# The start of a fused attention and feed-forward kernel rebuilt: two queues for q, column maxima of k by elementwise steps, exchanges on TensorE

## The chip, the cores and the metric

The kernel runs on one core of a Trainium2 chip. The metric is the device time of one execution in microseconds (us); three executions of the kernel before took 808.61, 810.38 and 810.49 us, so the median is 810.38.

## The reference

q, k and v are 8 batches x 8 heads x 576 rows x 64 columns. q goes through a softmax along its 64 columns, k through one along its 576 rows; for each batch and head the output is softmax(q) (softmax(k)ᵀ v). The heads are laid side by side, which gives x with 4608 rows of 512. Then out = softplus(x w_in) w_out with 2048 inner columns.

```python
q_s = softmax(q, axis=-1); k_s = softmax(k, axis=2)      # in fp32, with 1e-9 in the sums
kv  = einsum('bhsd,bhse->bhde', k_s, v)
x   = einsum('bhsd,bhde->bhse', q_s, kv)  ->  (4608, 512)
out = softplus(x @ w_in) @ w_out                          # (4608, 512)
```

## The kernel before

The 4608 rows are 9 tiles of 512. Tiles 0 to 2 go alone ("solo"): for each of 16 chunks j of the inner columns, U (line 720, `up`) makes a 512-wide product in PSUM with 12 matmuls, A (softplus, ScalarE) takes it out, G or H splits it into a high and a low part, and O (line 747, `down`) adds its product with w_out in 12 more matmuls. Every product is three matmuls, high x high, low x high, high x low. Chunks 0 and 1 of tile 0 are not split and go in plain fp32 (`up_whole`, line 707: tokens B and U1). Tiles 3 to 8 go as three pairs, by a scheme with 7 products for 8 (tokens C for the first matrix, e, t and d for the second). Weights come as 64-bit numbers and are decoded for each chunk: T and M (ScalarE), S, J and Q (mostly VectorE), P (ScalarE). Work on tile 0 can begin when q's softmax for it, and k's and v's part for batch 0, are done: that is the head, the part that the change rebuilds.

The order of everything is written out by hand: `ORDER` is a string of tokens, and `do` (line 1090) issues the instructions of each token as it comes. Each engine executes its own instructions in that order, and waits in place for what it needs. DMAs go mainly from SyncE's queue (SP), which is one line as well: a DMA that waits for a buffer holds up those behind it.

In the head before, SP loads q of tile 0 in four pieces of 64 partitions x 4 KB (`q_fetch`, line 555; z is the half of the partitions, g the pair of heads) and then the four k and v tiles of batch 0; their last 64 rows come from ScalarE's queue (`kv_load`, line 443). q (`q_unit`, line 570) takes a maximum over 32 columns, swaps the halves of each 64 over by four copies on ScalarE, and joins them for both pairs of heads at once; then it shifts, takes the exponential, sums, exchanges the sums by a matmul with the table `pair`, inverts and divides, half of each large step on VectorE and half on GpSimd. For k, `turn` (line 484) transposes the whole 128 x 10 x 64 tile on TensorE by ten matmuls into PSUM, and `across` takes the row maximum there with three VectorE steps. `spread` (line 506) sends the maximum back, `shift`, `power`, `product` and `scale` follow. The tokens w are matmuls on a table, with no use but to keep TensorE busy. Then q's transposes (`flip`, line 682), the product with kv (`x_product`, line 644), the copies to x0 (`take`, line 689), and U and O begin.

Of the kernel before, what the change touches and what calls it, by code (L numbers as in the profile page):

```python
# [7 lines left out]
F32 = mybir.dt.float32  # L8
# [11 lines left out]
P = 128  # L20
# [37 lines left out]
    k1.0.5 J4 U1 A0 k1.0.6 x0.2.3 k1.0.7 x0.2.4 O0 J3 P2 Q2 x0.0.3 x0.0.4 x0.1.3 T5 x0.3.3 x0.1.4 k1.1.1 x0.3.4 k1.1.2
    P3 Q3 A1 M5 k1.0.8 U2 T8 k1.1.3 k1.1.4 U3 P4 A2 q1.0 S5.1 T9 Q4 A3 G2 M6.1 O1 J5 G3 U4 k1.1.5 P5 O2 T6 M8.1 Q5.1
    k1.1.6 M7.1 T7 k1.2.0 k1.2.1 J6 J8 P6 k1.1.7 k1.2.2 q1.1 U5 A4 Q6 A5 J7 O3 U6 G4 G5 P7 M10 Q7 k1.1.8 O4 M9 q1.2  # L60
    T12 k1.3.0 U7 S9 q1.3 P8 A6 Q8 J9 T11 T10 A7 G6 q1.4 k1.3.1 O5 D4 P9 k1.2.3 G7 S10 M14.1 k1.2.4 q1.6 k1.3.2 O6
    M11.1 Q9 k1.2.5 U8 J11 A8 J10 P10 Q10 T14 U9 q1.8 A9 G8 M12.1 k1.2.6 k1.3.3 O7 P11 M13.1 Q11 J12 k1.3.4 G9 T13 P12
    q1.5 J13 q1.7 U10 Q12 J14 O8 U11 k1.3.5 A10 O9 k1.3.6 k1.2.7 U12 P13 A11 T15 Q13 q1.9 G10 q1.11 q1.10 P14 O10
    x1.0.0 A12 G11 U13 Q14 M15.1 k1.2.8 J15 x1.2.0 k1.3.7 P15 k1.3.8 Q15.1 U14 x1.1.0 A13 G12 D3 x1.1.3 O11 x1.3.0 U15
    G13 x1.0.4 x1.1.4 O12 x1.1.5 A14 x1.0.5 P0 Q0.1 k2.0.0 D6 G14 x1.3.3 D5 x1.2.4 k2.1.0 O13 x1.2.5 x1.3.4 P1 L2
    x1.3.5 D0 A15 Q1.1 G15 O14 k2.0.1 U16 k2.0.2 A16 D15 O15 U17 U18 A17 G16 k2.1.1 q2.1 Y0.1 k2.1.2 O16 G17 Y1.0 Y0.0
    q2.0 U19 k2.0.3 O17 A18 k2.1.3 k2.0.4 D1 G18 k2.1.4 Y0.2 D2 k2.0.5 q2.2 q2.3 Y1.2 D12 k2.1.5 Y2.1 A19 q2.5 O18
    Y1.1 D9 k2.1.6 k2.0.6 G19 D10 k2.0.7 q2.4.1 U20 Y2.0 Y2.2 n O19 U21 Y1.3 Y2.3 A20 Y0.3 D13 k2.0.8 Y2.4 Y2.5 G20
    Y1.4 O20 k2.2.0 U22 Y3.0 k2.1.7 A21 k2.2.1 D7 G21 k2.2.2 q2.6 q2.8 Y0.4 Y0.5 Y2.6 n D8 U23 q2.7 A22 k2.1.8 k2.2.3
    k2.3.0 Y3.2 O21 U24 G22 k2.3.1 k2.2.4 A23 q2.9 Y0.6 k2.3.2 A24 O22 q2.10 k2.3.3 k2.2.5 L3 Y1.5 H1.7.0 q2.11 x2.0.0  # L70
    D11 D14 k2.3.4 Y3.1 Y2.7 H1.7.1 U25 k2.2.6 k2.3.5 Y4.0 k2.2.7 Y2.8 k2.3.6 Y4.1 Y3.3 A25 Y1.6 O23 H1.8.0 U26 Y0.7
    k2.3.7 n A26 U27 Y3.4 x2.1.0 Y3.5 x2.2.0 H1.9.0 H1.8.1 O24 A27 Y3.6 H1.9.1 q3.0 O25 Y3.7 k2.3.8 k2.2.8 Y4.2
    H1.10.0 k3.0.0 n R0.0 Y3.8 H1.11.0 U28 k3.1.0 H1.10.1 x2.1.3 A28 q3.1 Y5.0 Y4.3 q3.12 x2.1.4 O26 Y0.8 Y4.4 k3.0.4
    H1.12.0 U29 q3.2 x2.1.5 U30 q3.3 k3.1.4 Y4.5 x2.0.4 H1.11.1 O27 x2.0.5 H1.12.1 A29 Y1.7 A30 U31 x2.3.0 H1.13.0
    x2.3.3 H1.13.1 k3.0.5 k3.1.5 q3.5 O28 q3.4 Y6.0 x2.3.4 Y7.1 R0.1 Y7.0 O29 x2.2.4 x2.2.5 R0.2 R0.3 q3.7 x2.3.5
    H1.14.0 Y6.1 L4 y0.1 H1.14.1 q3.6 A31 y0.0 R2.0 k3.1.6 Y7.2 k3.0.6 k3.0.7 Y1.8 Y6.2 Y4.6 q3.8 O30 H1.15.0 H1.15.1
    U32 n O31 n q3.13 y0.2 y1.0 A32 Y7.3 F1.0 Y4.7 U33 Y6.3 Y7.4 F1.2 Y6.4 q3.9 H2.0.0 k3.2.0 F1.3 y0.3 k3.3.0 R0.4
    y1.1 k3.2.4 A33 H2.1.0 U34 H2.0.1 F1.1 O32 k3.1.7 k3.2.5 k3.1.8 q4.0 q3.10 H2.1.1 y0.4 Y6.5 k3.0.8 y0.5 O33 k3.3.4
    A34 y1.2 k3.3.5 y2.0 k3.2.6 H2.2.0 Y4.8 q3.11 k3.3.6 H2.2.1 k3.2.7 U35 U36 R0.5 R0.6 y0.6 q4.1 Y7.5 A35 x3.1.0 n
# [131 lines left out]
def tile_attn_ffn(  # L211
# [249 lines left out]
    def kv_unit(b, h, bank):  # L461
# [10 lines left out]
        def top():  # L472
            if not b:
                return
# [95 lines left out]
    def q_unit(t):  # L570
# [48 lines left out]
        def invert():  # L619
            if t:  # L620
                if "s" not in state:
                    swap_all()
# [593 lines left out]
```

## Time and profile before

| | us |
|---|---|
| median of three executions | 810.38 |
| the profiled execution's own time | 809.8 |
| its span, first to last instruction | 808.0 |
| TensorE busy in the span | 795.7 (98%) |
| VectorE busy | 581.9 (72%) |
| ScalarE busy | 499.7 (62%) |
| GpSimd busy | 119.6 (15%) |

Names in the rows: PE is TensorE, DVE VectorE, ACT ScalarE, POOL GpSimd, SP SyncE; a q behind a name (SPq, ACTq) is its queue of DMAs. L with a number is the line of the kernel. `x` with a number is how many instructions a row merges. The duration of a row of several is from the first one's start to the last one's end. Instructions of one engine overlap at their ends, so the step from one start to the next is what an instruction costs in a row of them.

### The profile page before, as it was taken

How to read it: one execution, taken by the hardware profiler on the slowest of the kernel's cores; microseconds unless marked ns; L12 is line 12 of the kernel's file. 1: busy time of each engine (PE TensorE's matmuls, PEld its weight loads, DVE VectorE, ACT ScalarE, POOL GpSimd, SP SyncE). 2: the span in 40 equal slices, each digit the busy share in tenths (PEclk: the TensorE clock that was granted, in tenths of full speed). 3: DMA queues.
4: the chain of work that ended last, by engine and by line, in shares of the span. 5: the costliest groups of instructions: out<-in, count | busy, mean ns of one | idle time of the engine just before them, and what ended most of it. 6: DMA issues, size and time to landing. Idle time of an engine off the chain costs nothing.

```text
span 808.0 us, 12020 instructions
## 1 busy us (share of the span) xinstructions
PE 795.7 (98%) x4312; PEld 637.7 (79%) x4312; DVE 581.9 (72%) x934; ACT 499.7 (62%) x826; POOL 119.6 (15%) x211
## 2 busy tenths in 40 slices
PE   7999999999999999999999999999999999999997
PEld 6668877887787878878788778887777888888886
DVE  6979764877799878549689898477688943136884
ACT  2999964674577557557768574658466633336651
POOL 1320021101011210001010004240000220400026
PEclk9999999999999999999999999999999999999999
DMA  9996176869788898889789448994483865858655
GB/s 302 360 323 239 30 238 260 307 207 343 256 279 279 290 334 294 292 244 294 233 247 303 151 166 251 299 283 158 141 259 124 262 196 178 266 175 287 193 159 88
DMA packets 118235, 193.73 MB, mean 240 GB/s; under 512 B 8416, under 2 KB 90592, under 8 KB 108960
## 3 DMA queue, kind: packets, MB, share of 16 engines
q1 hardware_dynamic: 114912, 186.67, 70.0%
q0 software_dynamic: 2944, 6.04, 3.6%
q8 instruction: 34, 0.56, 0.3%
q10 hardware_dynamic: 320, 0.26, 0.1%
q14 instruction: 25, 0.20, 0.1%
HBM read 149.95 MB, written 42.99 MB: 239 GB/s over the span
## 4 chain that ended last, share of the span: by engine, by line
PE 94%; DMA 2%; ACT 1%; issue 1%; DVE 1%; POOL 0%; SPq 0%; DVEq 0%
PE po L965 7%; PE po L967 6%; PE po L966 6%; PE po L851 6%; PE po L853 6%; PE po L852 6%; PE po L766 5%; PE ph L724 5%; PE ph L725 5%; PE ph L726 5%; PE po L768 5%; PE po L767 5%; PE ph L851 3%; PE ph L853 3%; PE ph L852 3%; PE ph L965 3%
## 5 line engine op out<-in xcount | busy, mean ns | idle before, releaser
L1010 POOL DMA_DIRECT2D out<-w x92 | 59.4, 653 | 232.0 <-DVE w L1002 230.5
L766 PE MATMUL po<-w,g_hi 128*128 128x512 f32 x164 | 65.6, 400 | 0.0
L724 PE MATMUL ph<-x,w 128*128 128x512 f32 x164 | 65.3, 398 | 0.0
L945 ACT CAST g_hi<-w 128x512 fp32r<-128x512 f32 x74 | 45.8, 621 | 29.8 <-PE po L966 17.2
L768 PE MATMUL po<-w,g_lo 128*128 128x512 f32 x164 | 64.0, 390 | 0.0
L767 PE MATMUL po<-w,g_hi 128*128 128x512 f32 x164 | 64.0, 390 | 0.0
L726 PE MATMUL ph<-x,w 128*128 128x512 f32 x164 | 63.9, 390 | 0.0
L725 PE MATMUL ph<-x,w 128*128 128x512 f32 x164 | 63.9, 390 | 0.0
L948 DVE TENSOR_TENSOR g_lo<-w,g_hi 128x512 fp32r<-128x512 f32 x74 | 50.1, 684 | 11.4 <-ACT g_hi L945 11.1
L742 DVE TENSOR_TENSOR g_lo<-g,g_hi 128x512 fp32r<-128x512 f32 x46 | 32.7, 712 | 32.1 <-ACT g_hi L739 32.1
L733 ACT ACTIVATE g<-ph 128x512 f32<-128x512 f32 x48 | 28.6, 599 | 39.3 <-PE ph L726 39.1
L932 DVE TENSOR_TENSOR w<-w,w 128x512 f32<-128x512 f32 x72 | 47.5, 683 | 5.6 <-ACT w L885 5.6
L479 POOL PARTITION_ALL_REDUCE mx<-mx x20 | 23.0, 1150 | 189.6 <-DVE mx L476 186.4
L874 DVE TENSOR_TENSOR w<-po,w 128x512 f32<-128x512 f32 x24 | 16.3, 684 | 45.6 <-PE po L853 24.7
L945 ACT CAST w<-w 128x512 fp32r<-128x512 f32 x52 | 31.8, 619 | 22.5 <-PE po L966 14.8
L851 PE MATMUL po<-w,x 128*128 128x512 f32 x112 | 44.2, 394 | 0.3 <-DMA x<-sums 0.3
L852 PE MATMUL po<-w,x 128*128 128x512 f32 x112 | 43.6, 389 | 0.0
L853 PE MATMUL po<-w,x 128*128 128x512 f32 x112 | 43.6, 389 | 0.0
L948 DVE TENSOR_TENSOR w<-w,w 128x512 fp32r<-128x512 f32 x52 | 35.3, 684 | 10.9 <-ACT w L945 10.7
L739 ACT CAST g_hi<-g 128x512 fp32r<-128x512 f32 x46 | 28.3, 620 | 21.2 <-PE po L767 14.0
L476 DVE TENSOR_REDUCE mx<-kvt 128x128 f32<-128x640 f32 x28 | 36.7, 1312 | 5.6 <-DMA kvt<-in_kv_tail 4.4
L766 PEld LDWEIGHTS po<-w,g_hi 128*128 128x128 f32 x164 | 30.8, 188 | 10.2 <-issue 1.7
(380 smaller groups left out, 2253.2 us busy)
## 6 DMA issues: line engine op xcount, KB each, us to landing
x<-sums SPq DMA_DIRECT2D x24, 1024.0 KB, 5.6
kvt<-in_kv SPq DMA_DIRECT2D x30, 512.0 KB, 6.8
kept<-w SPq DMA_DIRECT2D x15, 1024.0 KB, 8.8
w<-kept SPq DMA_DIRECT2D x13, 1024.0 KB, 7.1
x<-sums_out SPq DMA_DIRECT2D x44, 256.0 KB, 4.3
w<-kept SPq DMA_DIRECT2D x36, 256.0 KB, 5.4
x<-kept SPq DMA_DIRECT2D x36, 256.0 KB, 4.8
w<-sums_out SPq DMA_DIRECT2D x36, 256.0 KB, 5.3
```

The lines of the kernel that those rows point to most:

```text
L724: nc.tensor.matmul(ph, lhsT=w_hi, rhs=x_hi, start=h == 0, stop=False)
L725: nc.tensor.matmul(ph, lhsT=w_lo, rhs=x_hi, start=False, stop=False)
L726: nc.tensor.matmul(ph, lhsT=w_hi, rhs=x_lo, start=False, stop=h == HP - 1)
L766: nc.tensor.matmul(po, lhsT=g_hi[:, ms], rhs=w_hi, start=j == 0, stop=False)
L767: nc.tensor.matmul(po, lhsT=g_hi[:, ms], rhs=w_lo, start=False, stop=False)
L768: nc.tensor.matmul(po, lhsT=g_lo[:, ms], rhs=w_hi, start=False, stop=j == NJ - 1)
L851: nc.tensor.matmul(ph, lhsT=w_hi, rhs=x_hi, start=c == 0 and i in (0, 4), stop=False, **more)
L852: nc.tensor.matmul(ph, lhsT=w_lo, rhs=x_hi, start=False, stop=False, **more)
L853: nc.tensor.matmul(ph, lhsT=w_hi, rhs=x_lo, start=False, stop=c == 1, **more)
L945: nc.scalar.copy(ring[p, i, s][0], right_of(p, i, s))
L948: engine.tensor_tensor(out=lo, in0=right_of(p, i, s), in1=hi.bitcast(F32), op=ALU.subtract)
L965: nc.tensor.matmul(bank, lhsT=w_hi, rhs=hi, start=begin, stop=False, **more)
```

## The change

- q of tile 0: the pieces of the upper 64 partitions (z = 1) go on ScalarE's queue, those of the lower on SP's.
- A new `q_first` for tile 0: each step by pairs of heads (g = 0, 1), with the halves of the maximum exchanged by a matmul with a new table `other_half` into PSUM, where four ScalarE copies did it.
- k's column maximum for batch 0: three elementwise maxima over the five chunks (two at a time, then the two results, then the last 64 rows), one 128 x 128 transpose on TensorE, and one row maximum. The ten matmuls of `turn` are gone.
- The inverses of k's sums are made for two heads at a time.
- The eight fills of batch 0's padding go from VectorE to GpSimd, ahead of GpSimd's first computing instruction, which has a token (g) of its own now.
- `ORDER` is written anew from the first token to the last. The token w stands for 25 table matmuls now (9, 5, 2, 5, 4) and 38 before (20, 5, 6, 7). The main products, their number and shapes, are the same.

```diff
-    w0.20 b0 b1 q0.0 n k0.0.1 n q0.1 n n q0.2 q0.3 q0.4.1 l0 q0.5 l1 k0.0.2 k0.1.1 l2 k0.1.2 k0.0.3 k0.2.1 k0.0.4
+    w0.9 b0 b1 n n n n g q0.0 q0.1 q0.2 q0.3 q0.4 w1.5 k0.0.0 q0.6 k0.0.1 q0.5 k0.1.0 l0 q0.7.1 k0.1.1 k0.0.2 k0.2.0
...
+    other_half = const.tile([P, P], F32, name="other_half")
...
+        nc.vector.tensor_tensor(out=other_half, in0=pair, in1=ident, op=ALU.subtract)
...
         def top():
+            mx = state["mx"] = sm.tile([P, 2, D], F32, name="mx", bufs=3)
             if not b:
+                two = sm.tile([P, 2, 2, D], F32, name="two")
+                for o, i0, i1 in (
+                    (two, kt[:, 0:2], kt[:, 2:4]), (mx, two[:, 0], two[:, 1]), (mx[0:TAIL], mx[0:TAIL], kt[0:TAIL, NCH]),
+                ):
+                    nc.vector.tensor_tensor(out=o, in0=i0, in1=i1, op=ALU.max)
                 return
...
         def turn():
-            if not b:
-                for c in range(NCH, -1, -1):
-                    rows = P if c < NCH else TAIL
-                    for z in range(2):
-                        zs = slice(z * D, (z + 1) * D)
-                        nc.tensor.matmul(
-                            bank[zs, c * P:(c + 1) * P] if c < NCH else rest[zs], lhsT=kt[0:rows, c, z],
-                            rhs=ident[0:rows, 0:rows], start=True, stop=True,
-                        )
-                return
             nc.tensor.transpose(wide, state["mx"].rearrange("p z d -> p (z d)"), ident)
...
+            if not b:
+                if h % 2:
+                    r = sm.tile([P, 2], F32, name=f"r{h // 2}")
...
-                nc.sync.dma_start(out=qtiles[t][z * D:(z + 1) * D, 2 * g:2 * g + 2], in_=src[z, g])
+                queue = nc.sync if t or not z else nc.scalar
+                queue.dma_start(out=qtiles[t][z * D:(z + 1) * D, 2 * g:2 * g + 2], in_=src[z, g])
...
+    def q_first():
...
+        def top(g):
+            nc.vector.tensor_reduce(out=m[:, g], in_=half[g], op=ALU.max, axis=AX.X)
+
+        def cross(g):
+            nc.tensor.matmul(sums[:, (2 + g) * n:(3 + g) * n], lhsT=other_half, rhs=m[:, g], start=True, stop=True)
+
+        def join(g):
+            nc.vector.tensor_tensor(out=m[:, g], in0=m[:, g], in1=sums[:, (2 + g) * n:(3 + g) * n], op=ALU.max)
...
-        nc.gpsimd.tensor_tensor(out=first, in0=first, in1=first, op=ALU.add)
...
-                place = dict(engine=nc.vector, queue=nc.scalar) if ahead[0] < HP else {}
+                place = dict(queue=nc.scalar) if ahead[0] < HP else {}
```

The first place is VectorE from q's maxima on. `m` and `qt` are q's, `kvt` and `x0` the k and v tiles, `po` and `ph` PSUM. Before:

```order
L580 TENSOR_REDUCE m_154<-qt_121 128x32
L450 MEMSET x0_178 64x2x64
L451 MEMSET x0_178 64x2x64
L450 MEMSET x2_183 64x2x64
L451 MEMSET x2_183 64x2x64
L591 TENSOR_TENSOR m_154<-m_154,other_188 128x64
L594 TENSOR_TENSOR qt_121<-qt_121,m_154 128x1024
L500 TENSOR_REDUCE m1_203<-ph1_128 128x1
L501 TENSOR_TENSOR po0_124<-po0_124,m1_203 128x1
L504 TENSOR_REDUCE m1_203<-po0_124 128x1
```

The same place now, where both of q's maxima come first:

```order
L645 TENSOR_REDUCE m_165<-qt_122 128x32 x2
L651 TENSOR_TENSOR m_165<-m_165,ph0_130 128x32
L483 TENSOR_TENSOR two_178<-kvt_144 128x256
L483 TENSOR_TENSOR mx_177<-two_178 128x128
L483 TENSOR_TENSOR mx_177<-mx_177,kvt_144 64x128
L654 TENSOR_TENSOR qt_122<-qt_122,m_165 128x1024
L651 TENSOR_TENSOR m_165<-m_165,ph0_130 128x32
L483 TENSOR_TENSOR two_186<-kvt_149 128x256
L483 TENSOR_TENSOR mx_185<-two_186 128x128
L483 TENSOR_TENSOR mx_185<-mx_185,kvt_149 64x128
L498 TENSOR_REDUCE m1_195<-po0_125 128x1
```

The fills have left VectorE, and k's maxima stand in it ahead of the transposes where they stood behind.

The second place is SP's queue around the first k and v tile of batch 1, which needs a buffer of batch 0 back. Before:

```order
L284 DMA w2_217<-in_w_in 128x512
L285 DMA w2_217<-in_w_out 128x512
L284 DMA w3_252<-in_w_in 128x512
L285 DMA w3_252<-in_w_out 128x512
L454 DMA kvt_369<-in_kv 128x8x128
L458 DMA kvt_369<-in_kv_tail 64x2x128
L284 DMA w4_415<-in_w_in 128x512
```

And now:

```order
L287 DMA w2_251<-in_w_in 128x512
L288 DMA w2_251<-in_w_out 128x512
L457 DMA kvt_286<-in_kv 128x8x128
L461 DMA kvt_286<-in_kv_tail 64x2x128
L287 DMA w3_300<-in_w_in 128x512
L288 DMA w3_300<-in_w_out 128x512
L287 DMA w4_326<-in_w_in 128x512
```

The weights of chunk 3 stand behind the waiting k and v tile now.

The third place is ScalarE from the first copy of x0 on. Before:

```order
L691 COPY x1_123<-po0_124 128x512
L542 ACTIVATE kvs0_91<-po3_127,r_406 64x64 x2
L691 COPY x1_123<-po1_125 128x512
L691 COPY x1_123<-po2_126 128x512
L304 ACTIVATE w2_217<-w2_217 128x1024
L312 ACTIVATE w3_252<-w3_252 128x1024
L306 ACTIVATE w3_252<-w3_252 128x1024
L312 ACTIVATE w4_415<-w4_415 128x1024
```

And now:

```order
L740 COPY x1_124<-po0_125 128x512
L545 ACTIVATE kvs0_91<-po3_128,r1_375 64x64 x2
L545 ACTIVATE kvs0_91<-po2_127,r1_375 64x64 x2
L740 COPY x1_124<-po1_126 128x512
L315 ACTIVATE w3_300<-w3_300 128x1024
L309 ACTIVATE w3_300<-w3_300 128x1024
L740 COPY x1_124<-po2_127 128x512
L315 ACTIVATE w4_326<-w4_326 128x1024
```

The third copy of x0 stands behind two decode steps of chunk 3 now.

## Rows read from the trace of the kernel before

**Rows 1.** The page: span, and section 1 (busy us, share, instructions).

```profile
span 808.0 us, 12020 instructions
...
PE 795.7 (98%) x4312; PEld 637.7 (79%) x4312; DVE 581.9 (72%) x934; ACT 499.7 (62%) x826; POOL 119.6 (15%) x211
```

**Rows 2.** TensorE's waits, whole span: who waited for whom, us, times, longest.

```profile
PE ph L1163 <- DVE ident L260: 3.0, 1, 3.0
PE ph L490 <- DVE m L500: 1.9, 1, 1.9
PE att L527 <- issue: 1.3, 1, 1.3
...
PE po L851 <- DMA x<-sums: 0.3, 1, 0.3
```

**Rows 3.** TensorE in order of time: start, us, line, operation, [idle before].

```profile
27.70 1.83 PE L1163 MATMUL ph<-ident 128*128 128x128 f32 x14
29.46 2.23 PE L650 MATMUL po<-w,kvs 64*64 64x512 f32 x12
...
44.67 0.48 PE L724 MATMUL ph<-x,spare 128*128 128x512 f32 x1
```

**Rows 4.** VectorE in order of time, the head.

```profile
6.39 1.22 DVE L580 TENSOR_REDUCE m<-qt 128x32 f32<-128x1024 f32 x1 [2.86 <-DMA qt<-in_q]
...
9.86 1.22 DVE L580 TENSOR_REDUCE m<-qt 128x32 f32<-128x1024 f32 x1 [1.59 <-DMA qt<-in_q]
...
12.14 0.22 DVE L591 TENSOR_TENSOR m<-m,other 128x64 f32<-128x64 f32 x1 [0.40 <-ACT other L567]
...
14.07 0.69 DVE L504 TENSOR_REDUCE m<-po 128x1 f32<-128x512 f32 x1
...
19.82 0.81 DVE L511 TENSOR_TENSOR x<-x,po 128x640 f32<-128x640 f32 x1
20.55 1.21 DVE L600 TENSOR_REDUCE s<-qt 128x32 f32<-128x1024 f32 x1
21.68 0.21 DVE L500 TENSOR_REDUCE m<-ph 128x1 f32<-128x64 f32 x1
...
25.58 0.55 DVE L626 RECIPROCAL s<-s 128x64 f32<-128x64 f32 x1
...
27.84 1.29 DVE L684 STREAM_TRANSPOSE w<-qt 128x512 f32<-128x512 f32 x2
...
35.03 0.29 DVE L504 TENSOR_REDUCE m<-att 128x1 f32<-128x128 f32 x1 [0.42 <-PE att L495]
```

**Rows 5.** Stretches: length, busy (count) of PE, PEld, DVE, ACT, POOL; PEclk, DMA share, GB/s.

```profile
6.00:8.00 2.00, 2.00 (x14) 2.00 (x14) 1.54 (x4) 0.00 (x0) 0.00 (x0) 1.00 1.04 229
14.00:15.00 1.00, 1.00 (x14) 0.93 (x14) 0.85 (x3) 0.72 (x1) 1.00 (x1) 0.56 1.04 414
...
40.00:60.00 20.00, 20.00 (x101) 13.15 (x102) 14.84 (x19) 19.90 (x27) 5.38 (x5) 1.00 1.06 330
60.00:80.00 20.00, 20.00 (x102) 16.46 (x98) 19.07 (x26) 19.57 (x24) 0.58 (x4) 1.00 0.70 247
```

**Rows 6.** ScalarE in order of time: q's swap and two decode steps of weights.

```profile
11.11 1.00 ACT L567 COPY other<-m 32x64 f32<-32x64 f32 x4 [9.08 <-DVE m L580]
...
20.58 1.15 ACT L312 ACTIVATE w<-w 128x1024 uint32<-128x1024 uint8 x1
21.61 1.14 ACT L304 ACTIVATE w<-w 128x1024 f32<-128x1024 f32 x1
```

**Rows 7.** SyncE's queue in order of time: q's four loads, first kvt of batch 1.

```profile
0.75 2.81 SPq L560 DMA_DIRECT2D qt<-in_q  x4
...
22.26 0.58 SPq L454 DMA_DIRECT2D kvt<-in_kv  x1
```

**Rows 8.** GpSimd in order of time: its first computing instruction, and q's shift.

```profile
9.49 0.18 POOL L1065 TENSOR_TENSOR first<-first 128x1 f32<-128x1 f32 x1 [8.65 <-issue]
12.45 2.95 POOL L594 TENSOR_TENSOR qt<-qt,m 128x1024 f32<-128x1024 f32 x1 [2.77 <-DMA kvt<-in_kv]
```

More of the change, by code (lines that the diff above doesn't have):

```diff
@@ L58 @@
[L58 to L67, printed above, removed]
@@ L459, in kv_load @@
         return t
+    inverse = {}
     def kv_unit(b, h, bank):
@@ L465, in kv_unit @@
         wide, ps = bank[:, 0:P], (bank[:, 0:D + 1] if b else bank[:, P:P + D])
-        total = ps[:, D:D + 1] if b else banks[h % 2][:, h // 2:h // 2 + 1]
-        rest = warm[:, P + D * h:P + D * (h + 1)]
+        total = ps[:, D:D + 1] if b else banks[h // 2][:, h % 2:h % 2 + 1]
         state = {}
@@ L604, in swap @@
         def swap(g):
-            if not t:
-                nc.tensor.matmul(sums[:, 0:2 * n][:, g], lhsT=pair, rhs=s[:, g], start=True, stop=True)
-                return
             if not other:
@@ L619, in invert @@
         def invert():
-            if t:
-                if "s" not in state:
-                    swap_all()
-                nc.vector.scalar_tensor_tensor(out=s, in0=s, scalar=EPS, in1=other[0], op0=ALU.add, op1=ALU.add)
-            else:
-                nc.vector.tensor_scalar(out=s, in0=sums[:, 0:2 * n], scalar1=EPS, scalar2=None, op0=ALU.add)
+            if "s" not in state:
+                swap_all()
+            nc.vector.scalar_tensor_tensor(out=s, in0=s, scalar=EPS, in1=other[0], op0=ALU.add, op1=ALU.add)
             nc.vector.reciprocal(s, s)
@@ L633, in q_unit, with spread, shift, power @@
             lambda: total(0), lambda: total(1), invert, lambda *e: divide(0, *e), lambda *e: divide(1, *e),
-        ] + ([cross, swap_all] if t else [lambda g=g: swap(slice(g * n, (g + 1) * n)) for g in range(2)])
+            cross, swap_all,
+        ]
+    def q_first():
+        n = TOK // 16
+        half = [qtiles[0][:, 2 * g:2 * g + 2].rearrange("p h (i r) -> p (h i) r", r=32) for g in range(2)]
+        m, s = (sm.tile([P, 2, n], F32, name=name) for name in ("m", "s"))
+        def spread(a, g):
+            return a[:, g].unsqueeze(2).broadcast_to([P, n, 32])
+        def top(g):
[4 more added lines that the diff above has]
+            nc.vector.tensor_tensor(out=m[:, g], in0=m[:, g], in1=sums[:, (2 + g) * n:(3 + g) * n], op=ALU.max)
+        def shift(g, engine=nc.vector):
+            engine.tensor_tensor(out=half[g], in0=half[g], in1=spread(m, g), op=ALU.subtract)
+        def power(g):
+            nc.scalar.activation(half[g], half[g], AF.Exp)
+        def total(g, on_pe=None):
+            if on_pe is None:
+                nc.vector.tensor_reduce(out=s[:, g], in_=half[g], op=ALU.add, axis=AX.X)
+                return
+            for e in range(32):
+                nc.tensor.matmul(
+                    sums[:, g * n:(g + 1) * n], lhsT=pair, rhs=half[g][:, :, e], start=e == 0, stop=e == 31
+                )
+        def swap(g):
+            nc.tensor.matmul(sums[:, g * n:(g + 1) * n], lhsT=pair, rhs=s[:, g], start=True, stop=True)
+        def invert(g):
+            nc.vector.tensor_scalar(
+                out=s[:, g], in0=sums[:, g * n:(g + 1) * n], scalar1=EPS, scalar2=None, op0=ALU.add
+            )
+            nc.vector.reciprocal(s[:, g], s[:, g])
+        def divide(g, engine=nc.vector):
+            engine.tensor_tensor(out=half[g], in0=half[g], in1=spread(s, g), op=ALU.mult)
+        return [
+            lambda *e, g=g, f=f: f(g, *e)
+            for f in (top, cross, join, shift, power, total, swap, invert, divide) for g in range(2)
+        ]
     def x_part(t, h):
```

305 lines of the change are left out of this document (159 added, 146 removed).

## The prediction, made before the changed kernel ran

> **What bounds the kernel now.** I read the page first: TensorE is busy 795.7 us of a span of 808.0 [rows 1], so no more than 12.3 us of the span can be won without fewer or faster matmuls, and the change takes away none of the main products. Then the list of TensorE's waits [rows 2], to see where the idle time lies: 3.0 us before the very first table matmul, 1.9 us in the head for a row maximum of k, and in the whole rest of the kernel single waits of 1.3 and 0.3 us and some smaller ones. Then TensorE in order of time [rows 3]: at 27.70 it still runs table matmuls, which are counted as busy and give nothing; the first product that is of use for x starts at 29.46, and the first split product (U of chunk 2) at 44.67. So the head is worth 29 us in which TensorE does little, and the rest is one dense stream behind it. What the head gains or loses shifts that stream, as long as the other engines can feed it. What feeds it in the head is VectorE: from q's second half [rows 4], at 9.86, to the first pair of q's transposes (27.84 and 1.29 long) it works almost without a pause.
>
> **The change part by part.** I follow VectorE's path from A, the landing of q's second half, to the end of the first two transposes, since TensorE's first product waits for them. Before, that is 9.86 to 29.13, or 19.3 us, with A at about 9.8.
>
> A itself: q moves 4 pieces of 256 KB, each to 64 partitions. While q alone moves, the queue gives 229 GB/s with the DMA engines all busy, and with whole tiles of 128 partitions 414 GB/s [rows 5], at 6 to 8 and at 14 to 15 us. Now two queues send the lower and the upper half together. q and the first two k tails are 1.18 MB; from about 2.5 us on this takes 2.8 us at 414 and 5.1 us at 229, so A lies between 5.3 and 7.6, and at 9.8 if the last pieces straggle as they do now. I take 7.0. The four issues on SP take 2.81 us [rows 7] and are two and two on two queues now, which helps q's second half by up to 1.4 us of it, and the k and v tiles behind them.
>
> The Trainium skill, DMA: Bandwidth & Descriptors, section Issuing engines are not separate DMA queues, says that DMAs from several engines share the same 16 DMA engines and that a second issuer saves issue time alone. By that rule A stays above 9; this is a rival below. [...]
>
> The path from A, in VectorE's new order. q's second maximum 1.22 [rows 4]. The exchange by TensorE has no row: at best nothing, at worst the 1.05 that the four ScalarE copies and their handover cost (from 11.11 [rows 6] to 12.14 [rows 4]); I take 0.35, since it is one small matmul, and 0.22 for the join. Shift of q's first half 1.13 (the step of 128 x 1024 from one start to the next, 20.55 to 21.68) and the second join 0.2. Four column maxima of k: each 256, 128 and 128 columns; the nearest rows are 0.22 at 64 columns (12.14) and 0.69 at 512 (14.07, a reduction), so by a line between them 0.4, 0.3 and 0.3, or 1.0 together; at the ends 0.7 and 2.1 a head. Four row maxima of 128 columns 0.25 each (0.29 at 35.03, less the overlap). Four shifts of k at 0.73 (19.82 to 20.55), two sums at 1.13, two inversions at 0.55 (25.58), one scale for two heads 0.35, q's division 1.15, two transposes 1.29. Sum: 1.22 + 0.57 + 1.13 + 0.2 + 4.0 + 1.0 + 2.92 + 2.26 + 1.1 + 0.35 + 1.15 + 1.29 = 17.2 us. That is 2.1 less than before: the fills and the waits for TensorE's ten transposes go, k's maxima by VectorE come in.
>
> What could make VectorE wait on this path: the k and v tiles, 2.36 MB at 414 GB/s, land between A + 1.4 and A + 5.7 and are wanted at A + 1.8 to A + 7.3. GpSimd's shift of q's second half takes 2.95 us [rows 8] and is wanted, with ScalarE's exponential behind it, 6.3 us after the second join; that needs 4.7 with a k exponential in between. GpSimd's first computing instruction now starts at 9.49 after 8.65 us of idling [rows 8]; with eight fills of about 0.17 ahead it is ready near 11, and is wanted at A + 4.1 = 11.1. So A below 7 gains less than it seems, until 1.6 us of reserve are used.
>
> With A = 7.0 the transposes end at 24.2 and the first product starts at 24.5 where it started at 29.46. From there to U of chunk 2 it was 15.2 us of gapless work [rows 3], 29.46 to 44.67. The same work comes now, with waits: the second pair of transposes ends 4.0 us after the first (decode of w0 1.13, scale 0.35, a maximum of 1.2 and the transposes 1.29), and ScalarE gives x0's third copy behind two decode steps of 1.03 each (the step from 20.58 to 21.61 [rows 6]). TensorE has some 4 us for that (half the product, four table matmuls, two fp32 products); I put 0.9 us for idling there. U of chunk 2 then starts at 40.6: 4.1 us earlier. I take 0.5 off for handovers, of which the new path has two more between VectorE and TensorE (VectorE idles 0.40 at one now, 12.14 in [rows 4]). That leaves 3.6.
>
> Behind the head the new order is another one everywhere, with no row for its waits. The waits of the body are 2.4 us now (of which [rows 2] show the two kinds). They can go to nothing or double; the distance in matmuls from the last reader of a buffer to the first use of what is fetched into it is, at its shortest, the same 6.8 us of TensorE work for the sums of weights in both orders, so I take no change. The tail has the same steps in nearly the same order: no change.
>
> The sum is against the profiled execution: 809.8 - 3.6 = 806.2. The median of the three is 810.38, 0.6 above it, so I forecast **806.3 us**.
>
> **The rivals.** First, the second queue moves nothing faster. For it: the DMA engines show a share of 1.04 while q moves, so they look full already [rows 5]. Against it: the same share gives 414 GB/s with other tiles. Then A is about 9.2, the chain still gains 2.1, and less 0.9 and 0.5 as above the total is 1.3 us: 808.5.
>
> Second, ScalarE gives the gain back. It is busy 19.90 and 19.57 of 20 us in the two stretches from 40 to 80 us [rows 5], decoding weights; an earlier TensorE would then wait for it. Against it: ScalarE's own chain begins with q's and k's exponentials, which move up as well, and it has no more to do than before save for two issues, as four copies of q leave it. If all but its 0.5 us of idle time is given back: 809.3.
>
> Third, TensorE's granted clock. It is at 0.56 from 14 to 15 us [rows 5], mostly the lower level of 1.2 GHz, behind a stretch with little TensorE work, and nothing there waits for TensorE's speed. With 25 table matmuls for 38, and ten for each k tile gone, such a stretch may lie on the first products at 24.5. A clock at half over the 3.3 us of them costs up to 1.7: 807.9. The Trainium skill, TensorE: Matmul & The Clock Gate, section HAM oscillation, says that idle gaps bring the low clock; the trace agrees in its one such stretch.
>
> Fourth, on the other side: SP's queue. The k and v tile of batch 1 waits for TensorE's first product on k to give the buffer back (issued at 22.26 now [rows 7]), and the weights of chunk 3 stand behind it in the queue now, where they stood ahead. ScalarE's decode of them stands ahead of x0's third copy, so a late chunk 3 stops U of chunk 1, and the rest with it. By my walk the buffer is free at about 16 and chunk 3 lands 6 to 7 us later, near 23, where it is wanted at 27.7: a reserve of 4.7. It decides once the buffer comes after 21; from there each us late is a us lost, and if it comes at 27, 6 us are lost beside the 3.6 gained, plus the clock that falls in the wait: 813.5. Against it: even the old order had it free at 22.26.
>
> **How the numbers follow.** Chances: the forecast 0.54, no faster transfer 0.14, ScalarE 0.12, the clock 0.10, SP's queue 0.10. The low end takes A at 5.8 (805.0) and some of the body's waits gone: 804.3. The high end reaches over the second rival, 810.0. Faster by over 0.3%, about what a measurement of this kernel can tell from no change, is below 807.9: nearly all of the forecast, half of the clock's case and a part of the first: 0.62. Slower is above 812.8: SP's queue and the body's new waits, 0.12. The rest, 0.26, is within 0.3%.
>
> **What the profile after would show.** Right: the first maximum of q's second half near 7.0, the first x product at 24 to 25, U of chunk 2 at 40 to 41.5, and from there no wait of TensorE longer than about 1 us. Wrong: the maximum after 9 (first rival); U of chunk 2 early but waits of TensorE for ScalarE's casts before 90 us (second); a granted clock of 0.5 between 24 and 32 (third); SP's issue of batch 1's first k and v tile after 21, and TensorE waiting for x0 (fourth). A few single waits of 1 to 3 us behind 100 us would make the forecast wrong without touching any step of the head.

## The result: 1% slower, and the profile after

The changed kernel took 818.99 us in the median of six runs (813.14 to 821.56); the kernel before took 810.24 beside it (808.40 to 810.49). The ratio is 1.0106, 95% interval 1.0069 to 1.0143: slower by about 1%, where I had forecast 806.3 us. The profiled execution took 816.54 us. The page after, span and section 1, against [rows 1]:

```profile
span 814.5 us, 11869 instructions
...
PE 796.2 (98%) x4214; PEld 636.4 (78%) x4214; DVE 587.3 (72%) x930; ACT 517.8 (64%) x836; POOL 116.2 (14%) x219
```

TensorE executes 98 instructions fewer and is busy as long as before (796.2 against 795.7 us). TensorE's waits over the whole span, to be held against [rows 2]:

```profile
PE ph L1211 <- DVE ident L262: 3.3, 1, 3.3
PE ph L900 <- DMA w<-kept: 3.2, 1, 3.2
PE ph L648 <- DVE m L645: 3.1, 1, 3.1
PE po L494 <- DVE mx L483: 2.7, 1, 2.7
PE po L501 <- DVE m L498: 0.6, 1, 0.6
```

Four of the five are in the head. The second is new and is not: one wait of 3.2 us for weights fetched back from memory. TensorE in order of time, the head and that place, against [rows 3]:

```profile
19.25 1.23 PE L516 MATMUL att<-one,kvt 128*64 128x1 f32 x20
20.34 1.31 PE L521 MATMUL po<-kvt 128*64 128x64 f32 x20
...
28.84 0.70 PE L516 MATMUL att<-one,x 128*64 128x1 f32 x20
29.39 0.78 PE L521 MATMUL po<-x 128*64 128x64 f32 x20
30.10 1.09 PE L699 MATMUL po<-w,kvs 64*64 64x512 f32 x8
...
45.32 0.82 PE L773 MATMUL ph<-x,spare 128*128 128x512 f32 x1
...
528.52 0.50 PE L900 MATMUL ph<-w,w 128*128 128x512 f32 x1 [3.22 <-DMA w<-kept]
```

The first product of x starts at 30.10 (29.46 before) and U of chunk 2 at 45.32 (44.67): the head gained nothing and lost 0.65 us. The same products of k take 1.23 and 1.31 us at 19 us and 0.70 and 0.78 at 29. The stretches tell why (length, busy and count of PE, PEld, DVE, ACT, POOL; granted clock, DMA share, GB/s):

```profile
7.00:10.00 3.00, 0.61 (x5) 0.50 (x4) 0.76 (x2) 0.00 (x0) 0.00 (x0) 1.00 1.02 308
10.00:12.00 2.00, 1.34 (x6) 1.34 (x7) 1.24 (x4) 0.00 (x0) 0.00 (x0) 0.65 1.06 279
20.00:24.00 4.00, 4.00 (x62) 3.82 (x62) 3.97 (x7) 3.80 (x5) 0.47 (x3) 0.50 0.61 222
24.00:28.00 4.00, 4.00 (x45) 3.82 (x41) 2.53 (x7) 3.11 (x5) 0.00 (x0) 0.54 0.99 296
...
524.90:528.50 3.60, 0.40 (x2) 0.00 (x0) 1.70 (x3) 2.56 (x7) 2.37 (x6) 1.00 1.09 351
528.50:533.00 4.50, 4.48 (x29) 3.33 (x30) 4.30 (x6) 0.00 (x0) 1.33 (x3) 0.62 0.72 251
```

TensorE was nearly idle from 7 to 10 us, and the granted clock is at the lower level, 1.2 GHz, from inside the next stretch until nearly 28 us; so the products for two of the four k and v tiles run at it, and those for the other two, at 27.6 and 28.8 us, do not. Behind the wait at 528 it falls once more. The loss of the profiled run adds up from this: 0.65 at chunk 2, 3.2 for the wait and about 1.7 for the low clock behind it (4.5 us at 0.62). That is 5.6 of the 6.5 us by which the last 512-wide product starts later (809.21 against 802.71); the rest is small. VectorE in the head, against [rows 4]:

```profile
9.39 1.22 DVE L645 TENSOR_REDUCE m<-qt 128x32 f32<-128x1024 f32 x1 [2.24 <-DMA qt<-in_q]
11.34 0.19 DVE L651 TENSOR_TENSOR m<-m,ph 128x32 f32<-128x32 f32 x1 [0.73 <-PE ph L648]
...
11.89 0.29 DVE L483 TENSOR_TENSOR mx<-two 128x128 f32<-128x128 f32 x1
...
14.10 2.04 DVE L483 TENSOR_TENSOR mx<-two 128x128 f32<-128x128 f32 x1
...
25.39 0.82 DVE L505 TENSOR_TENSOR x<-x,po 128x640 f32<-128x640 f32 x1 [1.03 <-PE po L501]
...
28.21 1.24 DVE L733 STREAM_TRANSPOSE w<-qt 128x512 f32<-128x512 f32 x2
```

And GpSimd, against [rows 8]:

```profile
14.09 1.91 POOL L654 TENSOR_TENSOR qt<-qt,m 128x1024 f32<-128x1024 f32 x1
```

The same maximum of 128 x 128 takes 0.29 us at 11.89 and 2.04 at 14.10, and ends as GpSimd's subtraction ends. q's second half is there at 9.39, hardly earlier than 9.86.

The head of the kernel before is not the same in each run either. In its profiled run the transposes of k meet a low clock from 14 to 17.5 us, and VectorE waits for them:

```profile
14.08 1.97 PE L490 MATMUL po<-ident,kvt 128*64 128x128 f32 x16
16.09 0.17 DVE L501 TENSOR_TENSOR po<-po,m 128x1 f32<-128x1 f32 x1 [1.20 <-PE po L490]
```

Experiment e2_body has the same head, and in its profiled run the same 16 matmuls take 1.09 us, the first product of x starts at 27.79 and U of chunk 2 at 43.02, 1.65 us earlier than in the run that the prediction was made from (q's second half was there 0.49 us earlier). So a difference of one or two microseconds between the heads of two profiled runs is not yet one between the kernels.

### The profile page after: what moved, and what is told of

The parts are those of the page before. It is cut to its first block, busy times and chain, and to the rows that moved or that the text cites. A ratio compares the mean times of both kernels' runs of the same rounds, so it can differ in the third digit from the quotient of the medians.

```text
span 814.5 us, 11869 instructions
## 1 busy us (share of the span) xinstructions
PE 796.2 (98%) x4214; PEld 636.4 (78%) x4214; DVE 587.3 (72%) x930; ACT 517.8 (64%) x836; POOL 116.2 (14%) x219
## 4 chain that ended last, share of the span: by engine, by line
PE 92%; DVE 3%; DMA 3%; ACT 1%; issue 1%; SPq 0%; DVEq 0%; ACTq 0%
PE po L1014 7%; PE po L1016 7%; PE po L1015 7%; PE po L900 6%; PE po L901 6%; PE po L902 6%; PE po L815 5%; PE ph L773 5%; PE ph L774 5%; PE po L816 5%; PE ph L775 5%; PE po L817 5%; PE ph L900 3%; PE ph L901 3%; PE ph L902 3%; PE ph L1014 3%
## 5 line engine op out<-in xcount | busy, mean ns | idle before, releaser
L997 DVE TENSOR_TENSOR g_lo<-w,g_hi 128x512 fp32r<-128x512 f32 x74 | 50.3, 686 | 17.2 <-ACT g_hi L994 16.4
L791 DVE TENSOR_TENSOR g_lo<-g,g_hi 128x512 fp32r<-128x512 f32 x46 | 36.0, 784 | 24.8 <-ACT g_hi L788 24.8
L927 DVE TENSOR_TENSOR w<-po,g 128x512 f32<-128x512 f32 x24 | 16.4, 686 | 45.3 <-PE po L902 43.9
L488 POOL PARTITION_ALL_REDUCE mx<-mx x20 | 20.3, 1014 | 198.6 <-DVE mx L485 191.5
L994 ACT CAST w<-w 128x512 fp32r<-128x512 f32 x52 | 32.1, 620 | 18.1 <-PE po L1015 15.2
```

The source lines that it names most:

```text
L994: nc.scalar.copy(ring[p, i, s][0], right_of(p, i, s))
L997: engine.tensor_tensor(out=lo, in0=right_of(p, i, s), in1=hi.bitcast(F32), op=ALU.subtract)
```

## The experiments

Each was timed beside the kernel before on the same chip; the kernel before took 809.0 to 810.9 us there. Lines that the diffs show are tokens of `ORDER` unless they are code.

**e1_head: the changed head, the old order behind it.** To U2 the tokens are those of the changed kernel; then follow, in the order of the kernel before, all that are left.

```diff
 A1 x0.3.3 Q3 T5 x0.3.4 U2
-M5 P4 k1.1.1 U3 O1 A2 G2 S5.1 Q4 A3
+k0.0.7 k0.2.7 k1.0.7 k1.1.1 k1.1.2 M5 k1.0.8 T8 k1.1.3 k1.1.4 U3 P4 A2
...
```

> The changed head, to the products of chunk 2 (token U2), and behind it the order of the kernel before. Theory 'order behind the head': the loss sits in the new order of the rest, at the fetch that TensorE waits 3.2 us for at 528 and the half clock that follows it (some 5 us of the 6.5 of the profiled run), so this kernel comes out at the head's own balance, 810.5 to 812 us, about 0.65 us above before at the first products of chunk 2 and no more behind them. Rival 'late head': the weights that land 3 us later and TensorE's 17 us at the half clock delay all that follows, so it takes 815 us or more whichever order stands behind it.

Measured: 812.20 us (811.04 to 815.68), ratio 1.0017 [1.0000, 1.0034]. The loss of 1% is gone with the new order. In the profiled run the head was slower than the changed kernel's (chunk 2 at 48.92, 4.25 us behind the kernel before and not the 0.65 expected, since the matmuls ran at the half clock's durations up to 34 us), and little was added behind: the distance to the kernel before is 5.2 us at 66 us and 5.8 at the end. So the rival, 815 us or more, falls; late weights cost at most 1.0 us there and do not go on costing.

**e2_body: the old head, the new order behind it.**

```diff
 P3 Q3 A1 M5 k1.0.8 U2
-T8 k1.1.3 k1.1.4 U3 P4 A2 q1.0 S5.1 T9 Q4 A3
+P4 U3 O1 A2 G2 S5.1 Q4 A3 U4 M6.1 J5
...
```

> The head of the kernel before, to the products of chunk 2 (token U2), and behind it the new order. Theory 'order behind the head': 814 to 819 us, with a wait of TensorE for a fetched weight between 480 and 540 us and the half clock behind it. Rival 'late head': 809 to 811 us, as before, and no single wait of TensorE above 1.5 us behind 100 us.

Measured: 815.70 us (811.20 to 819.07), ratio 1.0048 [1.0023, 1.0073]. The wait is there with the old head as well (line numbers are one higher than in the kernel before):

```profile
27.79 2.23 PE L651 MATMUL po<-w,kvs 64*64 64x512 f32 x12
...
43.02 0.48 PE L725 MATMUL ph<-x,spare 128*128 128x512 f32 x1
...
525.29 0.50 PE L852 MATMUL ph<-w,w 128*128 128x512 f32 x1 [2.96 <-DMA w<-kept]
```

The new order alone makes the kernel slower, and the wait is at the place named. The profiled run was the fastest of the ten, 811.20, with the wait in it: TensorE was 1.65 us ahead of the kernel before at chunk 2 and is 1.4 us behind it at the end, so the new order cost 3.05 us behind chunk 2, which is the wait. The half clock that was expected behind the wait did not come (granted clock 1.00 from 525.3 to 530 us, and a matmul every 0.23 us). That the slower runs, up to 819.07, lose the rest by a longer wait or a low clock at this place is not shown, since none of them was profiled.

**e3_fetch: one fetch ahead of one load.**

```diff
+R3.4.1
 L8 C1.0.15 C1.2.4 q7.3 k7.1.5 q7.5 C1.3.7 q7.4 q7.6
...
 q7.7 o0.store.1.1
-R3.4.1
 C1.3.8 C1.3.4
```

> The changed kernel with one token moved: the fetch of chunk 4's inner weight for the second pair of tiles (R3.4.1) stands just ahead of the load of q's tile 8 (L8), so its transfer queues ahead of q's four. Theory 'one late fetch': the wait of 3.2 us at 528 and the half clock behind it (1.7 us) go, the profiled run takes 811 to 812.5 us, the median falls by 4 to 6 us to 813 to 815, and the runs lie closer together. Rival 'full queue': the transfers between 505 and 530 us are late together (output stores and fetches share the DMA engines), so another fetch or q's tile 8 takes the place of this one: no change within 1.5 us, with a wait of 2 us or more within 15 us of the old one.

Measured: 812.94 us (811.20 to 817.37), ratio 1.0041 [1.0021, 1.0061], where e4_one_queue on the same chip, which leaves this place alone, took 818.61. TensorE's waits between 480 and 560 us are one:

```profile
PE ph L900 <- DMA x<-sums: 0.3, 1, 0.3
```

One token of 2312 is worth 5.7 us of the 7.7 by which e4_one_queue exceeded the kernel before. What had made the fetch late is seen in the changed kernel's DMAs from 495 to 535 us (KB each, median us from issue to landing), and in SyncE's queue:

```profile
out<-w POOLq DMA_DIRECT2D x28, 64.0 KB, 6.5
...
w<-kept SPq DMA_DIRECT2D x3, 512.0 KB, 11.3
...
qt<-in_q SPq DMA_DIRECT2D x4, 256.0 KB, 12.1
```

```profile
510.04 3.43 SPq L564 DMA_DIRECT2D qt<-in_q  x4
513.56 0.66 SPq L379 DMA_DIRECT2D spare<-kept  x1
514.26 4.79 SPq L373 DMA_DIRECT2D w<-kept  x2
```

The fetch was issued at 514.26 and landed at 528.48, 14.2 us later. In the kernel before the same fetch landed 7.9 us after its issue, at 519.86, and TensorE used it at 523.78. There q's four pieces stand just ahead of it as well, so they alone are not what is new; SyncE's queue and GpSimd's, before:

```profile
509.21 2.70 SPq L560 DMA_DIRECT2D qt<-in_q  x4
511.95 4.22 SPq L370 DMA_DIRECT2D w<-kept  x2
```

```profile
507.90 0.65 POOL L1010 DMA_DIRECT2D out<-w  x1 [0.55 <-DMA out<-w]
523.18 2.57 POOL L1010 DMA_DIRECT2D out<-w  x4 [14.63 <-DVE w L1002]
```

The output stores of the first pair pause while the fetch is under way in the kernel before. In the changed kernel 19 of them, of 64 KB each, are issued from 508.3 to 528.5, and two fetches of 256 KB (`spare`, at 509.39 and 513.56) stand around q's pieces. The DMA engines are full in both. e3_fetch takes 1.25 MB out of the fetch's way (q's pieces and one `spare`) and that is enough; which share of the delay the stores have is not shown. With q's tile 8 behind the fetch nothing waits for q. The expected time of the profiled run was missed (816.0), since its head had the longer stretch of the half clock (chunk 2 at 48.21).

**e4_one_queue: q's first tile on one queue again.**

```diff
-                queue = nc.sync if t or not z else nc.scalar
+                queue = nc.sync
```

> The changed kernel with all four pieces of q's first tile on SyncE's queue, as before. Theory 'the second queue carries nothing faster': the second half of q is there at 9.3 to 9.9 us as with two queues (9.39), and the first product of x starts within 0.5 us of 30.1 us. Rival 'two queues help and something else took the gain': the second half comes 1.5 us or more later than 9.39, and the first product of x is 1 us or more later than 30.1 us.

Measured: 818.61 us (816.04 to 821.04), ratio 1.0103 [1.0070, 1.0135], as with two queues. The second half is there at 9.21 and the first product of x at 29.67:

```profile
9.21 1.22 DVE L645 TENSOR_REDUCE m<-qt 128x32 f32<-128x1024 f32 x1 [1.30 <-DMA qt<-in_q]
```

The second queue does not bring the second half earlier; the first half comes at 6.69 where two queues brought it at 5.92, which made no product of x earlier (30.10 with two queues). By the Trainium skill, SBUF — State Buffer, section "Can I just issue two DMAs to hit both halves?", two transfers to the two halves are not fused and gain 6%; these runs agree (the last piece gains nothing).

**e5_warm and e6_warm_head: more matmuls on the table.** In e5 on the changed kernel, in e6 on e1_head.

```diff
-w0.9
+w0.19
...
+w5.8
 k0.1.1
```

> The changed kernel with more matmuls on the table of ones where TensorE has nothing else: 19 instead of 9 at the start, and 8 ahead of head 1's turn. Theory 'half clock': the k products (1.23 and 1.31 us a group at the half clock, 0.70 and 0.78 at the full one) and the table's matmuls set VectorE's last subtraction of k, which waits 1.03 us for them at 25.4; with the full clock from 10 to 24 us the first product of x starts 2 to 3 us earlier than 30.1, chunk 2 (45.3) at 42.5 to 43.5, and the time falls by 2 to 4 us against the changed kernel's 818.99, to 815 to 817. Rival 'VectorE sets the head': the clock is full and the first product of x still starts within 0.5 us of 30.1, the time is 818 to 820. Second rival: the clock is half all the same.

> The same matmuls added to the changed head, and from chunk 2 on the order of the kernel before (as in e1_head, 812.2 us). Theory 'half clock': 807.5 to 809.5 us, under the kernel before by 1.5 to 3.5. Rival 'VectorE sets the head': 811 to 813 us, as e1_head.

Measured: e5 817.82 us (815.26 to 820.85), ratio 1.0110 [1.0074, 1.0147]; e6 813.66 (810.82 to 815.29), ratio 1.0035 [1.0017, 1.0053]. Neither the theory's time nor that of the first rival came, in either run; e5's second rival, that the clock is half all the same, is what both traces show. In e5 the matmuls are quick up to 19.5 us and slow behind it:

```profile
18.92 0.77 PE L516 MATMUL att<-one,kvt 128*64 128x1 f32 x20
19.54 1.32 PE L521 MATMUL po<-kvt 128*64 128x64 f32 x20
```

TensorE had stood for 1.85 and 1.14 us for VectorE between 14 and 18.4 us, and the low clock came after those waits instead. The first product of x came at 29.24 and chunk 2 at 44.58, 0.7 us earlier than in the changed kernel. In e6 the low clock came from 16.8 us on, chunk 2 started at 45.07, and a wait of 0.44 us for decoded weights stands at 56 us. Filling some of the gaps moved the fall of the clock and didn't prevent it.

**e7_shift: q's second subtraction on VectorE.**

```diff
-q0.7.1
+q0.7
```

> The changed kernel with the subtraction from q's second half on VectorE in place of GpSimd (1.21 us on VectorE; beside GpSimd's 1.91 us VectorE's maximum took 2.04 us instead of 0.29). Theory 'VectorE stands still while GpSimd runs': the maximum takes 0.29 us again, the k path behind it is 0.4 to 0.8 us earlier, and the first product of x 0 to 0.8 us earlier than 30.1 where the clock falls and rises as in the profiled run; the time moves by less than 1 us (818 to 820). Rival 'the maximum waits for its data': it takes 2 us with GpSimd idle as well, and the first product of x comes 0.5 us or more later.

Measured: 817.82 us (816.35 to 819.68), ratio 1.0099 [1.0074, 1.0123]. VectorE at the same place:

```profile
14.12 0.29 DVE L483 TENSOR_TENSOR mx<-two 128x128 f32<-128x128 f32 x1
```

The maximum takes 0.29 us again, so it was GpSimd's subtraction beside it that held VectorE for 1.75 us. The Trainium skill, SBUF — State Buffer, section Who interferes with whom, says that an instruction of VectorE with two inputs in SBUF contends with one of GpSimd that reads SBUF, and that the one issued second is blocked; the trace agrees, for GpSimd's began at 14.09 and VectorE's at 14.10. Before, VectorE's came first, and GpSimd's took 2.95 us [rows 8]. The first product of x came at 29.02, 1.1 us earlier (the matmuls are quick again from 26 us on and not from 27.7, so not all of it is this). The time cannot be told from the changed kernel's: in the profiled run the wait for the fetch, now at 529, is 5.1 us.

**e8_before_fewer: the kernel before with the changed kernel's number of table matmuls.**

```diff
-w0.20
+w0.9
```

> The kernel before with 9 instead of 20 matmuls on the table of ones at the start, as many as the changed kernel has there; nothing else. Theory 'half clock': TensorE stands idle from 7 to 9.7 us, the clock is half for 10 us or more of the head, the products of k take 1.2 to 1.3 us a group instead of 0.70 and 0.78, the first product of x comes 1 to 4 us later than 29.46 and the time is 811 to 815 us. Rival 'the turns of k keep the clock': no more than the one short drop that the kernel before has at 14 us (3.4 us), and the time stays within 0.8 us of before.

Measured: 812.33 us (809.04 to 814.20), ratio 1.0017 [0.9999, 1.0034]: not told apart from no change in time. In the trace the turns of k run at the half clock's durations from 13 to 18 us (1.97 us for 16 matmuls, 1.09 at the full clock); the kernel before has its low stretch from 14 to 17.5. It ends before the products of k, the first product of x is at 29.47 and chunk 2 at 44.69, as before, though q's second half was there 0.69 us earlier (9.17). So the rival was right on the clock: nine matmuls on the table alone don't make the long low stretch; in the changed kernel the turns of k are gone as well. The time decides nothing: it is 1.45 us above the kernel before, where the rival had 0.8 at most, and inside the theory's 811 to 815, but not clear of no change. What the profiled run lost came later, in a wait for weights:

```profile
56.28 0.50 PE L725 MATMUL ph<-x,w 128*128 128x512 f32 x1 [1.91 <-DVE w L347]
```

**e9_weights_first: chunk 3's weights ahead of batch 1's k and v.**

```diff
 k0.2.5 k0.1.7
+l3
 n k0.1.8 w3.5 k0.3.4
-l3
```

> The changed kernel with the loads of chunk 3's weights (l3) issued ahead of batch 1's first tile of k and v (n), as the kernel before has them; nothing else. Theory 'queue of SP': the stretch from 20 to 24 us moves near 400 GB/s in place of 222, chunk 3's first weights land 2.5 to 3.5 us earlier than 28.18 and the last of the first pass (51.12) 2 to 4 us earlier; TensorE's start is held by the head and not by these loads, so the time stays within 1 us of the changed kernel's (818 to 820). Rival 'the late weights set the end': 815 to 817 us.

Measured: 818.02 us (816.64 to 821.14), ratio 1.0111 [1.0080, 1.0142]: no change, as expected. The gap in the loads is closed (the stretch, columns as above):

```profile
20.00:24.00 4.00, 4.00 (x64) 3.82 (x64) 3.97 (x7) 3.96 (x5) 0.47 (x3) 0.50 1.03 410
```

Chunk 3's first weights land at 23.75 (28.18 in the changed kernel; 4.4 us, more than expected) and the last of the first pass at 48.47 (51.12). SP's queue did stand still behind the k and v tile in the changed kernel (222 GB/s in this stretch), but in this head, at the half clock, TensorE did not need the weights earlier.

**e10_head_mended and e11_both: the three together.** In e10 before the old order, in e11 before the new one with the fetch of e3_fetch.

```diff
-w0.9
+w0.19
...
-q0.7.1
+q0.7 w5.5
...
+w6.3
 k0.0.3
-w2.2
+w2.4
...
+w7.2
 q0.12 q0.14
...
+l3
 n k0.1.8
-w3.5
+w3.3
...
```

> The changed head with three things mended at once: more matmuls on the table of ones in TensorE's waits, q's second subtraction on VectorE, chunk 3's weights ahead of batch 1's k and v; from chunk 2 on the order of the kernel before (as in e1_head, 812.2, and e6_warm_head, 813.66). Theory 'clock, stall and queue together': the clock is full from 5 to 30 us, the first product of x starts at 26.5 to 28 us (29.46 before), chunk 2 at 42 to 43.5, no wait of 1 us or more for weights between 45 and 66 us, and 806.5 to 809.5 us. Rival 'the loads set it': TensorE is as early, and waits as much longer for weights behind chunk 2, 810 to 812 us. Second rival: the clock falls all the same, 811 to 814 us.

> The same mended head before the new order of the rest, with the fetch of chunk 4's inner weight ahead of q's tile 8 (as in e3_fetch, 812.94 us). Theory 'the head and one fetch are all': 807 to 811 us, no wait of TensorE above 1.5 us behind 50 us. Rival 'the new order is slower in itself': 1.5 us or more above e10_head_mended.

Measured: e10 810.06 us (809.25 to 813.35), ratio 1.0016 [0.9999, 1.0034]; e11 810.62 (809.34 to 812.41), ratio 1.0013 [0.9999, 1.0027]. Neither can be told from the kernel before, and e11 contains the whole change with its order. TensorE in e10, the stretches of the head and the first product of x:

```profile
7.00:10.00 3.00, 2.86 (x25) 2.75 (x24) 0.92 (x2) 0.00 (x0) 0.00 (x0) 1.00 1.02 314
10.00:12.00 2.00, 1.49 (x12) 1.41 (x12) 1.43 (x5) 0.00 (x0) 0.00 (x0) 1.00 1.07 275
20.00:24.00 4.00, 3.27 (x58) 2.86 (x57) 3.93 (x9) 3.69 (x6) 0.26 (x2) 1.00 1.03 408
```

```profile
18.20 0.75 PE L516 MATMUL att<-one,kvt 128*64 128x1 f32 x20
...
27.04 1.09 PE L699 MATMUL po<-w,kvs 64*64 64x512 f32 x8 [0.32 <-ACT kvs L545]
...
29.92 1.13 PE L761 MATMUL ph<-x,w 128*128 128x512 f32 x2 [0.70 <-ACT x L740]
```

The first product of x starts 2.4 us earlier than in the profiled run of the kernel before, but chunk 2 only 1.3 (43.38): TensorE waits 0.7 us twice for ScalarE's copies of x0. At the end 0.6 us are left in the profiled runs (802.12 against 802.71 for the last 512-wide product), and none in the medians. Beside e2_body's profiled run, where the head of the kernel before has the full clock too, the mended head is 0.75 us earlier at the first product of x and 0.36 us later at chunk 2: in these two runs, with the full clock in both, the new head gains nothing for the stream behind it. The theory's time, 806.5 to 809.5, was not reached, nor was the weights' wait of the rival seen. The rival of e11 falls: the two orders behind the same head differ by less than 1 us. In e11 the clock fell all the same, later, over the last products of k and the first of x (chunk 2 at 43.78):

```profile
26.00:30.00 4.00, 3.99 (x50) 2.19 (x48) 3.97 (x7) 3.93 (x6) 2.38 (x4) 0.58 1.08 346
```

**e12_few_matmuls: e10 without the added matmuls.** As in e10, with `w0.9`, `w1.5`, `w2.2` and `w3.5` left as they are and no `w5`, `w6`, `w7`.

```diff
-q0.7.1
+q0.7
...
+l3
 n k0.1.8 w3.5 k0.3.4
-l3
```

> As e10_head_mended (810.06 us; first product of x at 27.04, chunk 2 at 43.38), without the added matmuls on the table of ones: 9, 5, 2 and 5 of them stand where the changed kernel has them. Theory 'half clock': TensorE runs at the half clock from about 11 us for 14 us or longer, the first product of x comes at 28.5 to 33 us, chunk 2 at 44.3 to 48, the time is 811 to 814 us and the runs lie further apart than the 4 us of e10_head_mended. Rival 'the stall and the queue were all': chunk 2 within 0.4 us of 43.38 and 809.5 to 810.5 us.

Measured: 810.94 us (809.59 to 814.20), ratio 1.0022 [1.0006, 1.0039]. The first product of x is at 28.93 and chunk 2 at 44.34, 1.0 us behind e10, and at the end 0.9 us behind it. Both starts lie in the theory's ranges, and the rival, chunk 2 within 0.4 us of 43.38, falls; the time is 0.06 us below the theory's 811 to 814 and cannot be told from e10's. The low clock of the head costs about 1 us here where a profile shows it. The runs fall into two groups: seven at 809.6 to 811.0 with a mean clock of 0.999 or 1.000, and five at 812.5 to 814.2 with 0.984 to 0.991. That the second group had a longer low stretch is not shown: no run of it was profiled, the profiled run has matmuls at the half clock's durations at a recorded clock of 1.00, and in e3_fetch the slowest run (817.37) has 0.999 and the fastest (811.20) 0.989.

## Why the prediction was wrong

**The step that failed first** is the one on the part behind the head: "I take no change". I had compared one kind of fetch, the sums of weights, in both orders, by its distance in matmuls alone, and left out the inner weights of the second matrix, which SyncE's queue carries behind q's tiles. There the old order has the same 1 MB of q ahead of the fetch, and a landing 7.9 us after the issue, 3.9 us before it is used; the new order adds two fetches of 256 KB around q and lets the output stores run at the same time, and the landing takes 14.2 us, 3.2 too many. e4_one_queue, the change but for one queue, is 7.7 us slower than the kernel before, and moving this fetch gives back 5.7 of them (e3_fetch); every kernel with the changed head and the fetch where it was stays at 818 (e4, e5, e7, e9), whatever was mended in the head alone. The prediction's last sentence named such waits, and its 0.12 for a slower kernel the body's new waits, but no term of the sum and no rival had them, and the range ended at 810.0.

**The head's gain of 3.6 us** was wrong in three of its terms, and came out at a loss of 0.65.

- The landing A: 7.0 forecast, 9.39 measured. My first rival had it (9.2), and e4_one_queue shows that the second queue changes nothing.
- The path from A to the first transposes: 17.2 forecast, 20.1 measured (9.39 to 29.45). The single durations were right: the three maxima of k take 0.42, 0.29 and 0.28, together 1.0 with no overlap. Missing were VectorE's 1.75 us beside GpSimd (shown by e7_shift), 1.03 and 0.37 us for TensorE at the half clock, and some 0.4 for the exchange, with its wait of 0.73 (together 3.5, of which 0.6 is hidden again by shorter steps than I had). In e10_head_mended, at the full clock and with the subtraction on VectorE, the first and both waits for the half clock are gone. The 19.3 us that I set against the path held waits for the low clock as well: in e2_body the old path takes 18.1 (9.37 to 27.45), so 1.2 of the 2.1 us that I counted as a gain came from that clock.
- From the transposes to chunk 2: 0.9 us of idling forecast. In the changed kernel there is hardly any, since TensorE came late; in e10_head_mended, where TensorE is early, it is 1.4 us for x0's copies. The 0.5 for handovers was not measured apart.

The forecast itself has a slip that changes nothing: 806.2 with the median 0.6 above it is 806.8, not 806.3.

**The rivals.** The clock was the third, with 1.7 us over the first products of x. The fall came earlier than I had put it, at 10.6 us, and lasted over the products of two of the four k and v tiles; its sign was right. The Trainium skill, TensorE: Matmul & The Clock Gate, section HAM oscillation, has idle gaps bring the low clock; the stretches from 7 to 12 us agree. The price of the low clock is 1.0 us between the profiled runs of e10 and e12; in those of e1_head and e3_fetch, where it lasted to 34 us, chunk 2 came 2.9 to 3.6 us later than in the changed kernel's. Two premises were wrong: that nothing at 14 us waits for TensorE's speed (VectorE waits 1.20 us there), and the price, for the first eight products of x, 1.09 us at the full clock, take 1.99 at the half one (e1_head), so that 3.3 us of them would lose some 2.7 by these rows, an estimate, and not 1.7. SP's queue was the fourth: the buffer did come back only at 21.75, past my limit of 21, as the products of k are late and slow; chunk 3's first weights landed at 28.18 (24.90 in the kernel before), but no wait of TensorE for x0 above 0.2 us came of it, and e9_weights_first shows that it cost nothing here. ScalarE, the second, shows only once the head is mended: the two waits of 0.7 us.

**What stays open:** whether e2_body lost less than the changed kernel at all (4.8 against 7.7 us for e4_one_queue beside the same runs of before; the intervals meet, and the new head alone, e1_head, costs 1.3), and how much of the runs' spread is the head's clock and how much is waits, or a low clock behind them, that the one profiled execution does not show. A kernel that holds back the output stores was not run.

## What to carry to other kernels

Where a new order is written for the whole kernel, walk every kind of fetch in each queue, not the one with the shortest distance: from the last reader to the issue, through all bytes queued ahead of it and those that other queues move meanwhile, to the first use. A load that nobody waits for can cost much where it stands ahead of one that is waited for. Before a gain is read off two profiled runs, see what the same code takes in a third. And work that is taken from an idle TensorE may have kept its clock: price what stands behind it at both levels.

## What the runs showed of the hardware

- Beside a GpSimd subtraction of 128 x 1024 (1.91 us), VectorE's maximum of two tiles in SBUF took 2.04 us instead of 0.29, and GpSimd was not slowed (its division of the same size, at 28.44 in the changed kernel, takes 1.92); with VectorE first, before, GpSimd took 2.95 us and VectorE's 1.22 was as always.
- The record of the granted clock can miss a low stretch. In e1_head, e7_shift and e12_few_matmuls it shows 1.00 throughout the head, and the first products of k take the time that they take at 0.50 in the changed kernel (e1_head, the stretch from 18 to 24 us, then two rows in order of time):

```profile
18.00:24.00 6.00, 5.43 (x75) 4.79 (x76) 5.90 (x13) 5.40 (x6) 0.47 (x3) 1.00 0.75 280
```

```profile
19.32 1.24 PE L516 MATMUL att<-one,kvt 128*64 128x1 f32 x20
20.41 1.31 PE L521 MATMUL po<-kvt 128*64 128x64 f32 x20
```

So the clock was most likely low there too, and the durations of a known instruction are the surer sign.
- The end of the low stretch is not the same in each run: 27.7 us in the changed kernel's profiled run, about 34 in those of e1_head and e3_fetch with the same head, which moved chunk 2 from 45.3 to 48.9 and 48.2 us. The head of the kernel before had a low stretch from 14 to 17.5 us in its own profiled run and none in e2_body's.
- A wait of 3 us was followed by the low clock in one run (3.22 us, 0.62 over the next 4.5) and not in another (2.96 us in e2_body, 1.00).
